# The second layer of eight tiles as seven products of quarters, in a fused attention and feed-forward kernel

## The chip, the cores and the metric

The kernel runs on one core of one Trainium2 chip. The time is device microseconds (us) of that core, the median over runs. The profile is one execution of the program, recorded on the chip; its lines give the engine (PE is TensorE's matmul, PEld its weight load, DVE VectorE, ACT ScalarE, POOL GpSimd, SP SyncE), the line of the kernel, the operation and its operands as "out<-in" by the program's names.

## The reference, cut to what matters

```python
def _attn_ref(q, k, v, g_norm):                 # q, k, v: 8 x 8 x 576 x 64
    kv = np.einsum('bhsd,bhse->bhde', k, v)
    out = np.einsum('bhsd,bhde->bhse', q, kv)
    rms = np.sqrt(np.mean(out * out, axis=-1, keepdims=True) + 1e-06)
    return out / rms * g_norm

def _moe_ref(x, w_in, w_out):                   # x: 4608 x 512, w_in: 512 x 2048, w_out: 2048 x 512
    h = x @ w_in
    g = h * (1.0 / (1.0 + np.exp(-1.702 * h)))
    return g @ w_out
```

The output of the attention, its heads side by side, is x: 8 batches of 576 rows with 512 columns. All of it is float32 outside; the kernel computes in float16 with float32 sums.

## The kernel before

**Tiles.** The 4608 rows go through the two layers in nine tiles of 512 rows: tile t (0 to 7) takes the first 512 rows of batch t, and tile 8 the 64 rows that are left of each of the eight batches, collected in `x_rem`. A tile has 16 blocks of 128 hidden columns. The first layer (`Hidden.mm`, L438) forms each block from four matmuls of 512 columns into a PSUM bank `hT`, and `gate` (L447, ScalarE) writes it as float16 into `gT`. The second layer (`project`, L475) then forms four blocks of 128 output rows, each from 16 matmuls: the weights loaded are a 128x128 piece of `gT`, the moving side is a row block of `w_out_sb` with 512 columns. So a tile is 64 matmuls and 64 matmuls. The bank of a finished block is copied to `osb` (L485) by ScalarE or VectorE and stored from there. In tile 8 the fourth block is split into 384 and 128 columns (`project_last`, L507).

**What lies in between.** While tile t is computed, the attention of batch t+1 is prepared in small units that `at1` hangs behind a block of the first layer and `at2` behind a numbered step of the second. For batches 2 to 7 they are: `cast_q` and the DMA transposes of q (`transpose_q`), `pack_k` (VectorE, L218), `kv` (TensorE, L227) with `keep_kv` (VectorE, L240), all in the first layer; then, in the second, `rows(0..3)` (four matmuls of 128 columns each, L291, a square on ScalarE, L299, a sum on VectorE, L302), `turn(0)` and `turn(2)` (for two row blocks each: Ln and Exp on ScalarE, L312 and L313; two multiplications `xr` on VectorE, L316, reading the banks of `rows`; one multiplication by g each on GpSimd and VectorE, L323; a DMA transpose on SP, L328, that writes half of the next tile's input `xT`), and `out`, `ss`, `apply` for the 64 left rows (L270, L339, L357). Tile 0 has a form of its own (`deep`), and batch 1 is prepared there in another way; tiles 7 and 8 prepare nothing.

**What sets the order.** Each engine works through its instructions in the order in which the kernel writes them, so a unit's place is where `at1` and `at2` put it. PSUM has three pools with a rotation each: `ps_h` (3 banks: `hT`, and `rows` 0 to 2), `ps_o` (2 banks: `o`) and `ps_a` (3 banks: `kvp` twice a tile, `rows` 3, `out`, `ss`). The next tile that is asked of a pool gets the bank that was given out longest ago, and the first writer waits for that bank's last reader. `gT` has one buffer, `osb` two. ScalarE has two table loads per tile: L653 ahead of the first Ln, and L447 ahead of the first gate.

The loop over the second layer's steps before is

```python
steps = [(mo, fo) for mo in range(4 - (t == B)) for fo in range(FO)]
for n, (mo, fo) in enumerate(steps):
    project(mo, fo)
    for u in units2.get(n, ()):
        u()
```

Of the kernel before, what the change touches and what calls it, by code (L numbers as in the profile page):

```python
# [7 lines left out]
F16 = mybir.dt.float16  # L8
# [4 lines left out]
P = 128  # L13
# [3 lines left out]
def kernel(  # L17
# [21 lines left out]
    R = S - SM  # L39
    assert R == 64 and B * R == SM and KO == NPAIR and 2 * D == P  # L40
    NT = B + 1
    LAST = ((0, 3 * P), (3 * P, DM))
    EARLY = 2
    PE_ = 96
    NJ = S // PE_
# [8 lines left out]
    attn = ctx.enter_context(tc.tile_pool(name="attn", bufs=4))  # L54
    xpool = ctx.enter_context(tc.tile_pool(name="xpool", bufs=2))
    gpool = ctx.enter_context(tc.tile_pool(name="gpool", bufs=1))
    opool = ctx.enter_context(tc.tile_pool(name="opool", bufs=2))
    ps_a = ctx.enter_context(tc.tile_pool(name="ps_a", bufs=3, space=bass.MemoryType.PSUM))
    ps_h = ctx.enter_context(tc.tile_pool(name="ps_h", bufs=3, space=bass.MemoryType.PSUM))
# [10 lines left out]
    kbuf = const.tile([P, NPAIR * NJ * P], F16)  # L70
# [9 lines left out]
    w_in_sb = const.tile([P, KO, DFF], F16)  # L80
    w_out_sb = const.tile([P, FO, DM], F16)
    x_rem = const.tile([P, KO, B * R], F16)


    raw = {"k": kraw, "q": qraw, "v": vbuf}
# [55 lines left out]

    first = {}
    for n in "kqv":
        first[n] = stage.tile([P, H, J * D], F32, name=f"{n}f", tag=f"{n}f")
        first[n] = first[n].rearrange("p h x -> p (h x)")[0:PE_, 0 : 2 * NJ * D]
# [283 lines left out]
    class Hidden:  # L429
# [16 lines left out]
        def gate(self, fo):  # L446
            nc.scalar.activation(self.gT[:, fo, :], self.h[fo], AFT.Gelu_apprx_sigmoid)  # L447

    def dense(t, units1, units2, group, deep, hid=None):
        hid = hid or Hidden(t)  # L450
        gT = hid.gT
        if group and t:
            order = [(ko, fo) for part in ((0, 3, 1, 2), range(4, group)) for ko in (0, 1) for fo in part]
            order += [(ko, fo) for ko in range(2, KO) for fo in range(group)]
            for ko, fo in order:
                pool = (ps_h, "hT") if fo < 3 else (ps_a, "att") if fo == 3 else (ps_o, "o")
                hid.mm(ko, fo, *pool)
            for fo in range(group):
                hid.gate(fo)
        for fo in range(FO):  # L460
            if fo >= group:
                for ko in range(KO):
                    hid.mm(ko, fo)
                hid.gate(fo)
            for u in units1.get(fo, ()):
                u()

        osb = osbs[t] = opool.tile([P, 4, DM], F32, name="osb", tag="osb")
        os = {}

        def project(mo, fo):
            if fo == 0:
                pool, tag = (ps_h, "hT") if deep and mo < 2 else (ps_o, "o")
                os[mo] = pool.tile([P, DM], F32, name="o", tag=tag)
            nc.tensor.matmul(  # L475
                os[mo],
                gT[:, fo, mo * P : (mo + 1) * P],
                w_out_sb[:, fo, :],
                start=(fo == 0),
                stop=(fo == FO - 1),  # L480
            )
            if fo == FO - 1:
                by_act = mo % 2 if deep or t == B else 0 < t < B - 1 and mo < 2
                copy = nc.scalar.copy if by_act else nc.vector.tensor_copy
                copy(osb[:, mo, :], os[mo])  # L485
                if t == B:
                    store_rest(mo, 0, DM)
                elif t in HALVED and mo % 2:
                    store(t, mo - 1, mo + 1)

        def store_rest(mo, n0, n1):
            for g in range(2):
                rows = out[(2 * mo + g) * S : (2 * mo + g + 1) * S, n0:n1]
                if 2 * mo + g < EARLY:
                    p0 = SM % PE_
                    rows = rows[bass.DynSlice(NJ * p0 + SM // PE_, R, step=NJ), :]
                else:
                    rows = rows[SM:S, :]
                queue = (nc.sync, nc.scalar)[g]
                queue.dma_start(out=rows, in_=osb[g * R : (g + 1) * R, mo, n0:n1])  # L500


        def project_last(mo):
            for i, (n0, n1) in enumerate(LAST):
                o = ps_a.tile([P, n1 - n0], F32, name="oh", tag="att")
                for fo in range(FO):
                    nc.tensor.matmul(  # L507
                        o,
                        gT[:, fo, mo * P : (mo + 1) * P],
                        w_out_sb[:, fo, n0:n1],  # L510
                        start=(fo == 0),
                        stop=(fo == FO - 1),
                    )
                copy = nc.vector.tensor_copy if i else nc.scalar.copy
                copy(osb[:, mo, n0:n1], o)  # L515
                store_rest(mo, n0, n1)

        if deep:
            steps = [(mo, 4 * i + k) for i in range(3) for mo in range(4) for k in range(4)]
            steps += [(mo, f + k) for f in (12, 14) for mo in range(2) for k in range(2)]  # L520
            steps += [(mo, 12 + k) for mo in (2, 3) for k in range(4)]
        else:
            steps = [(mo, fo) for mo in range(4 - (t == B)) for fo in range(FO)]
        for n, (mo, fo) in enumerate(steps):
            project(mo, fo)
            for u in units2.get(n, ()):
                u()
        if t == B:
            project_last(3)
# [115 lines left out]
    for t in range(NT):  # L645
# [12 lines left out]
        if t == 0:  # L658
            at1(7, of(0, "out", NPAIR))
            at2(4, setattr, a0, "ss_pool", Attention.ss_pool)  # L660
            at2(4, of(0, "ss", NPAIR, True))
            at2(4, of(0, "apply", NPAIR))
            at1(8, start, 1)
            for l in range(2):
                r = slice(l * PH, (l + 1) * PH)
                at1(8, nc.vector.memset, kpad[r, :, :, (1 - l) * D : (2 - l) * D], 0.0)
            for c in range(NPAIR):
                at1(12, of(1, "pack_q", c))
                at2(9 + 3 * c, of(1, "q", c))
# [63 lines left out]
```

## Time and profile before

| what | value |
|---|---|
| median of 3 runs | 286.75 us (286.32 to 287.19) |
| span of the profiled execution, first to last instruction | 285.4 us |
| its own time beside the span | not recorded apart; the runs' median is 1.35 above the span |
| granted TensorE clock | 1.000 |
| PE busy; the second layer's matmuls (L475); the first layer's (L438) | 278.8; 130.8; 116.4 and 14.0 us |
| VectorE, ScalarE, GpSimd busy | 119.2, 156.0, 59.5 us |
| second layer, tiles 1 to 6, first start to the next tile's first | 14.9 to 15.2 us each |
| second layer, tile 7 and tile 8 | 13.8 us each |

A row of the groups gives the line, engine, operation and operands, the count, then busy us and the mean ns of one, then the idle time of that engine just before these operations and what ended most of it. A row of a timeline gives start and duration in us of one instruction, or of several of one kind in a row (xN); the distance between their starts is shorter than one's duration, since matmuls are pipelined. A matmul of 512 columns has a record of 379 ns, while 64 of them in a row take 13.98 us. A figure in square brackets is idle time of the engine before the instruction, with what it waited for.

### The profile page before, as it was taken

The numbers are of one execution on the slowest core, as the hardware profiler recorded it, in microseconds if no ns is written. First come the engines' busy times: TensorE is split into PE (matmuls) and PEld (weight loads), VectorE is DVE, ScalarE is ACT, GpSimd is POOL, SyncE is SP. The second block draws the span as 40 slices with busy tenths as digits, with TensorE's granted clock in tenths as the row PEclk, the third lists the DMA queues.
The fourth block names the chain that finished last, engine by engine and source line by source line (L and its number), as shares of the span: only waits on it lengthen the run. The fifth ranks groups of instructions, "written<-read, shape, count | busy, mean of one in ns | idle before, by whom it ended". The sixth has DMA issues, their size and how long they took to land.

```text
span 285.4 us, 4458 instructions
## 1 busy us (share of the span) xinstructions
PE 278.8 (98%) x1768; PEld 136.9 (48%) x1768; DVE 119.2 (42%) x230; ACT 156.0 (55%) x273; POOL 59.5 (21%) x86
## 2 busy tenths in 40 slices
PE   8899999999999999999999999999999999999995
PEld 6444544455445544554455445544454444444443
DVE  2550547627661657147713852286327400110001
ACT  2688439766575645574467536763666365016400
POOL 8762372111211121112011401130001100000000
PEclk9999999999999999999999999999999999999999
DMA  8999999998579456963798269915401410012022
GB/s 174 192 198 205 205 235 239 208 262 158 127 168 249 73 128 175 238 95 62 208 207 161 41 209 230 161 37 184 85 0 37 117 69 0 2 60 87 0 75 75
DMA packets 55158, 38.78 MB, mean 136 GB/s; under 512 B 31282, under 2 KB 52018, under 8 KB 55010
## 3 DMA queue, kind: packets, MB, share of 16 engines
q0 software_dynamic: 16048, 15.59, 33.8%
q1 hardware_dynamic: 38688, 22.39, 30.5%
q10 hardware_dynamic: 402, 0.52, 0.6%
q8 instruction: 14, 0.23, 0.3%
q14 instruction: 6, 0.05, 0.1%
HBM read 36.73 MB, written 9.44 MB: 162 GB/s over the span
## 4 chain that ended last, share of the span: by engine, by line
PE 83%; DMA 13%; POOL 2%; issue 0%; DVE 0%
PE hT L438 39%; PE o L475 38%; DMA w_out_sb<-in_moe_w_out_dram 7%; DMA w_in_sb<-in_moe_w_in_dram 5%; PE kvp L227 2%; PE outR L291 2%; PE oh L507 1%; POOL qraw L91 1%; PE ss L339 0%; POOL kraw L91 0%; POOL vbuf L91 0%; PE outT L270 0%; PE outT L259 0%; DVE osb L515 0%; POOL ident L152 0%
## 5 line engine op out<-in xcount | busy, mean ns | idle before, releaser
L475 PE MATMUL o<-w_out_sb,gT 128*128 128x512 f16 x560 | 130.8, 379 | 0.1
L447 ACT ACTIVATE gT<-hT 128x512 f16<-128x512 f32 x144 | 84.5, 601 | 75.8 <-PE hT L438 75.8
L438 PE MATMUL hT<-xT,w_in_sb 128*128 128x512 f16 x512 | 116.4, 379 | 0.8 <-DMA w_in_sb<-in_moe_w_in_dram 0.8
L438 PEld LDWEIGHTS <-w_in_sb 128*128 128x128 f16 x576 | 54.6, 98 | 63.1 <-DMA w_in_sb<-in_moe_w_in_dram 1.1
L475 PEld LDWEIGHTS <-gT 128*128 128x128 f16 x560 | 52.9, 98 | 56.6 <-issue 0.4
L485 DVE COPY osb<-o 128x512 f32<-128x512 f32 x20 | 13.8, 691 | 62.4 <-PE o L475 62.4
L323 POOL TENSOR_TENSOR x<-xr,g_all 128x512 f16<-128x512 f32 x12 | 15.3, 1272 | 70.4 <-DVE xr L316 46.3
L218 DVE COPY kpad<-kraw 64x576 f16<-64x576 f16 x56 | 25.0, 446 | 2.4 <-DMA kraw<-in_k_dram 1.1
L240 DVE CAST kvb<-kvp 64x128 f16<-64x128 f32 x28 | 8.1, 289 | 39.1 <-PE kvp L227 38.9
L302 DVE TENSOR_REDUCE sum<-sq 128x8 f32<-128x512 f16 x24 | 15.8, 679 | 19.1 <-ACT sq L299 19.1
L112 POOL DMA_DIRECT2D kraw<-in_k_dram x16 | 10.0, 626 | 50.0 <-DVE kpad L218 34.5
L316 DVE TENSOR_TENSOR xr<-outR,sum 128x512 f32<-128x512 f32 x24 | 15.5, 686 | 11.1 <-ACT sum L313 11.1
L112 POOL DMA_DIRECT2D vbuf<-in_v_dram x16 | 9.7, 609 | 32.0 <-PE kvp L227 27.0
L323 DVE TENSOR_TENSOR x<-xr,g_all 128x512 f16<-128x512 f32 x12 | 15.2, 1268 | 0.7
L279 ACT ACTIVATE sq<-outT 128x512 f16<-128x512 f32 (+1 forms) x16 | 7.7, 488 | 13.2 <-PE outT L259 11.8
L299 ACT ACTIVATE sq<-outR 128x512 f16<-128x512 f32 x24 | 13.6, 590 | 2.0 <-PE outR L291 1.6
L227 PEld LDWEIGHTS <-kpad 128*128 128x128 f16 x252 | 11.0, 98 | 6.7 <-issue 0.6
L438 PE MATMUL hT<-x_rem,w_in_sb 128*128 128x512 f16 x64 | 14.0, 379 | 0.0
L485 ACT COPY osb<-o 128x512 f32<-128x512 f32 x15 | 8.7, 582 | 6.3 <-PE o L475 6.3
L227 PE MATMUL kvp<-vbuf,kpad 128*128 128x64 f16 x252 | 11.9, 193 | 0.1
L312 ACT ACTIVATE sum<-sum,eps_t 128x16 f32<-128x16 f32 x12 | 3.7, 308 | 15.0 <-DVE sum L302 15.0
L341 ACT ACTIVATE ln<-ss,eps_t 128x512 f32<-128x512 f32 (+1 forms) x16 | 9.4, 585 | 2.7 <-PE ss L339 2.6
(64 smaller groups left out, 145.1 us busy)
## 6 DMA issues: line engine op xcount, KB each, us to landing
qf<-in_q_dram SPq DMA_DIRECT2D x5, 1024.0 KB, 9.5
out_dram<-osb SPq DMA_DIRECT2D x10, 512.0 KB, 2.9
kraw<-in_k_dram POOLq DMA_DIRECT2D x12, 288.0 KB, 6.7
vbuf<-in_v_dram POOLq DMA_DIRECT2D x12, 288.0 KB, 5.8
out_dram<-osb SPq DMA_DIRECT2D x6, 192.0 KB, 6.0
w_in_sb<-in_moe_w_in_dram POOLq DMA_DIRECT2D x4, 256.0 KB, 7.7
w_out_sb<-in_moe_w_out_dram POOLq DMA_DIRECT2D x2, 512.0 KB, 14.5
w_out_sb<-in_moe_w_out_dram POOLq DMA_DIRECT2D x4, 256.0 KB, 10.6
```

The source lines that it names most:

```text
L112: nc.gpsimd.dma_start(out=raw[n][l * PH : (l + 1) * PH, c0:c1, 0 : NH * D], in_=srcs[n][b].rearrange("(c l) (p j) d -> l p c (j d)", l=2, ...
L218: nc.vector.tensor_copy(out=kpad[r, c, :, l * D : (l + 1) * D], in_=kraw[r, c, 0 : NH * D].rearrange("p (j d) -> p j d", j=NH),)
L227: nc.tensor.matmul(self.kvp[:, c, :], kpad[:, c, j, :], vbuf[:, c, j * D : (j + 1) * D], start=(j == 0), stop=(j == NH - 1),)
L299: nc.scalar.activation(sq, t, AFT.Square)
L302: nc.vector.tensor_reduce(out=self.sum2[:, j % 2, :], in_=sq.rearrange("p (h d) -> p h d", h=H), op=ALU.add, axis=mybir.AxisListType.X,)
L316: nc.vector.tensor_mul(xr[:, i], self.o[j + i].rearrange("p (h d) -> p h d", h=H), s2[:, i, :].unsqueeze(2).to_broadcast([P, H, D]),)
L323: (nc.vector if i else nc.gpsimd).tensor_mul(self.x16[:, j + i, :].rearrange("p (h d) -> p h d", h=H), xr[:, i], g_all.unsqueeze(1).to_bro ...
L341: nc.scalar.activation(ln[:, 0:n], t[:, 0:n], AFT.Ln, bias=eps_t, scale=1.0 / D)
L438: nc.tensor.matmul(self.h[fo], w_in_sb[:, ko, fo * P : (fo + 1) * P], self.x[:, ko], start=(ko == 0), stop=(ko == KO - 1),)
L447: nc.scalar.activation(self.gT[:, fo, :], self.h[fo], AFT.Gelu_apprx_sigmoid)
L475: nc.tensor.matmul(os[mo], gT[:, fo, mo * P : (mo + 1) * P], w_out_sb[:, fo, :], start=(fo == 0), stop=(fo == FO - 1),)
L485: copy(osb[:, mo, :], os[mo])
```

## The change

In tiles 1 to 8 the second layer is computed by Strassen's scheme in Winograd's form. `gT` is cut into quarters (hidden blocks 0 to 7 and 8 to 15, rows 0 to 255 and 256 to 511), `w_out_sb` likewise (hidden blocks, and columns 0 to 255 and 256 to 511). Instead of eight products of quarters there are seven, each of 16 matmuls with 256 moving columns: 112 matmuls per tile. They need sums of quarters as operands. Those of `w_out` (`tw`, four of 128x2048) are formed once, on VectorE in tile 1 (`weight_sums`); those of `gT` (`gS`, four of 128x2048 per tile) on VectorE in three portions behind blocks 8, 12 and 15 of the first layer, whose blocks now come in the order 0, 8, 1, 9 and so on. The products go in the order 1, 5, 6, 2, 7, 3, 4 into three banks: x (products 1, 6, 7, 4, one on top of the other), z (5 and 3) and y (2). After products 1, 5 and 6 the partial sum is copied to SBUF by ScalarE (`s1`, `s5`, `s2`); after 2, 7 and 3 VectorE adds one of these copies to the bank and writes a quarter of the output; after 4 ScalarE copies the last quarter. x and z are from `ps_o`, y from `ps_a`, so that in tiles 2 to 6 a tile takes six banks from `ps_a` instead of five. A unit that hung behind step n now hangs behind step 7n/4, rounded down. In tile 8 x is two half tiles, one of them from `ps_a`, and the stores of a whole output row block follow products 7 and 3. In tile 0 the code of the second layer stays as it was. The first loads of q, k and v share two staging buffers, and an unused one (`kbuf`) goes.

```diff
-    LAST = ((0, 3 * P), (3 * P, DM))
+    spool = ctx.enter_context(tc.tile_pool(name="spool", bufs=1))
+    HF, HN = FO // 2, DM // 2
+    tw = const.tile([P, 4, HF, HN], F16)
...
+    def weight_sums():
+        b11, b12 = w_out_sb[:, 0:HF, 0:HN], w_out_sb[:, 0:HF, HN:DM]
+        b21, b22 = w_out_sb[:, HF:FO, 0:HN], w_out_sb[:, HF:FO, HN:DM]
+        sub = nc.vector.tensor_sub
+        sub(tw[:, 0], b12, b11)
+        sub(tw[:, 1], b22, tw[:, 0])
+        sub(tw[:, 2], b22, b12)
+        sub(tw[:, 3], b21, tw[:, 1])
...
+        def sums(self, i0, i1):
+            lo, hi = slice(i0, i1), slice(HF + i0, HF + i1)
+            r1, r2 = slice(0, 2 * P), slice(2 * P, SM)
+            g, s = self.gT, self.s
+            nc.vector.tensor_add(s[:, 0, lo], g[:, lo, r2], g[:, hi, r2])
+            nc.vector.tensor_sub(s[:, 1, lo], s[:, 0, lo], g[:, lo, r1])
+            nc.vector.tensor_sub(s[:, 2, lo], g[:, lo, r1], g[:, lo, r2])
+            nc.vector.tensor_sub(s[:, 3, lo], g[:, hi, r1], s[:, 1, lo])
...
+                1: (self.gT[:, i, rows], w[:, i, 0:HN]),
+                2: (self.gT[:, HF + i, rows], w[:, HF + i, 0:HN]),
+                3: (self.s[:, 3, i, rows], w[:, HF + i, HN:DM]),
+                4: (self.gT[:, HF + i, lower], tw[:, 3, i]),
+                5: (self.s[:, 0, i, rows], tw[:, 0, i]),
+                6: (self.s[:, 1, i, rows], tw[:, 1, i]),
+                7: (self.s[:, 2, i, rows], tw[:, 2, i]),
...
+                pool, tag = (ps_a, "att") if name == "y" or key[1] else (ps_o, "o")
+                n = 1 if split else 2
+                self.bank[key] = pool.tile([P, n, HN], F32, name="o7", tag=tag)
...
+        def keep(self, name, as_):
+            t = self.kept[as_] = attn.tile([P, 2, HN], F32, name=as_, tag=as_, bufs=1)
+            for ps, m in self.whole(name):
+                nc.scalar.copy(t[:, m], ps)
...
+                if with_:
+                    nc.vector.tensor_add(o[:, m], ps, self.kept[with_][:, m])
+                else:
+                    nc.scalar.copy(o[:, m], ps)
+                    if self.t == B:
+                        store_rest(2 * i + m.start, j * HN, (j + 1) * HN)
...
+        def run(self, units2):
+            n = 0
+            for p in self.ORDER:
+                name = {1: "x", 6: "x", 7: "x", 4: "x", 2: "y", 5: "z", 3: "z"}[p]
...
+                        if mo and i == HF - 1:
+                            self.after(p)
+                        for u in units2.get(n, ()):
+                            u()
+                        n += 1
...
+            if p == 1:
+                self.keep("x", "s1")
+            elif p == 5:
+                self.keep("z", "s5")
+            elif p == 6:
+                self.keep("x", "s2")
+            elif p == 2:
+                self.place("y", "s1", 0, 0)
+            elif p == 7:
+                self.place("x", "s5", 1, 1)
+                if t == B:
+                    store_rest(2, HN, DM)
+                    store_rest(3, HN, DM)
+            elif p == 3:
+                self.place("z", "s2", 0, 1)
+                if t == B:
+                    store_rest(0, 0, DM)
+                    store_rest(1, 0, DM)
+                elif t in HALVED:
+                    store(t, 0, 2)
+            else:
+                self.place("x", None, 1, 0)
+                if t in HALVED:
+                    store(t, 2, J)
...
+        seven = None if deep else Seven(t, gT)
+        cols = range(FO) if deep else [f for i in range(HF) for f in (i, HF + i)]
+        ready = {} if deep else {8: (0, 4), 12: (4, 6), 15: (6, 8)}
...
+            if i in ready:
+                seven.sums(*ready[i])
+            for u in units1.get(i, ()):
                 u()
...
+            later = {}
+            for n, us in units2.items():
+                later.setdefault(n * 7 // 4, []).extend(us)
+            seven.run(later)
...
             if t == 1:
+                at1(5, weight_sums)
```

More of the change, by code (lines that the diff above doesn't have):

```diff
@@ L69 @@
     qrem = [const.tile([P, 2, P], F16, name=f"qrem{i}") for i in range(2)]
-    kbuf = const.tile([P, NPAIR * NJ * P], F16)
     qbuf = const.tile([P, NPAIR * NJ * P], F16)
@@ L143 @@
     for n in "kqv":
-        first[n] = stage.tile([P, H, J * D], F32, name=f"{n}f", tag=f"{n}f")
-        first[n] = first[n].rearrange("p h x -> p (h x)")[0:PE_, 0 : 2 * NJ * D]
+        if n != "q":
+            rows = stage.tile([P, H, J * D], F32, name="qf", tag="qf")
+            rows = rows.rearrange("p h x -> p (h x)")[0:PE_]
+        first[n] = rows[:, (n == "q") * 2 * NJ * D :][:, 0 : 2 * NJ * D]
         dst, src = first[n].rearrange("p (h x) -> p h x", h=2), early_src(n, 0, 0, 1)
@@ L447, in gate, with __init__, operands, banks @@
             nc.scalar.activation(self.gT[:, fo, :], self.h[fo], AFT.Gelu_apprx_sigmoid)
+    def weight_sums():
[6 more added lines that the diff above has]
+        sub(tw[:, 3], b21, tw[:, 1])
+    class Seven:
+        ORDER = (1, 5, 6, 2, 7, 3, 4)
+        def __init__(self, t, gT):
+            self.t, self.gT = t, gT
+            self.s = spool.tile([P, 4, HF, 2 * P], F16, name="gS", tag="gS")
+            self.bank, self.kept = {}, {}
+        def sums(self, i0, i1):
[6 more added lines that the diff above has]
+            nc.vector.tensor_sub(s[:, 3, lo], g[:, hi, r1], s[:, 1, lo])
+        def operands(self, p, mo, i):
+            rows = slice(mo * P, (mo + 1) * P)
+            lower = slice((2 + mo) * P, (3 + mo) * P)
+            w = w_out_sb
+            return {
+                1: (self.gT[:, i, rows], w[:, i, 0:HN]),
[5 more added lines that the diff above has]
+                7: (self.s[:, 2, i, rows], tw[:, 2, i]),
+            }[p]
+        def banks(self, name, mo):
+            split = self.t == B and name == "x"
+            key = (name, mo if split else 0)
+            if key not in self.bank:
+                pool, tag = (ps_a, "att") if name == "y" or key[1] else (ps_o, "o")
+                n = 1 if split else 2
+                self.bank[key] = pool.tile([P, n, HN], F32, name="o7", tag=tag)
+            return self.bank[key][:, 0 if split else mo]
+        def whole(self, name):
+            return [
+                (self.bank[k], slice(k[1], k[1] + self.bank[k].shape[1]))
+                for k in sorted(self.bank)
+                if k[0] == name
+            ]
+        def keep(self, name, as_):
+            t = self.kept[as_] = attn.tile([P, 2, HN], F32, name=as_, tag=as_, bufs=1)
+            for ps, m in self.whole(name):
+                nc.scalar.copy(t[:, m], ps)
+        def place(self, name, with_, i, j):
+            o = osbs[self.t][:, 2 * i : 2 * i + 2, j * HN : (j + 1) * HN]
+            for ps, m in self.whole(name):
+                if with_:
[8 more added lines that the diff above has]
+                name = {1: "x", 6: "x", 7: "x", 4: "x", 2: "y", 5: "z", 3: "z"}[p]
+                split = self.t == B and name == "x"
+                for mo in range(2):
+                    o = self.banks(name, mo)
+                    for i in range(HF):
+                        a, w = self.operands(p, mo, i)
+                        nc.tensor.matmul(
+                            o,
+                            a,
+                            w,
+                            start=(p in (1, 2, 5) and i == 0 and (mo == 0 or split)),
+                            stop=(i == HF - 1),
+                            skip_group_check=True,
+                        )
+                        if mo and i == HF - 1:
[3 more added lines that the diff above has]
+                        n += 1
+        def after(self, p):
+            t = self.t
+            if p == 1:
[22 more added lines that the diff above has]
+                    store(t, 2, J)
@@ L449, in dense, with store_rest @@
+    def store_rest(mo, n0, n1):
+        osb = osbs[B]
+        for g in range(2):
+            rows = out[(2 * mo + g) * S : (2 * mo + g + 1) * S, n0:n1]
+            if 2 * mo + g < EARLY:
+                p0 = SM % PE_
+                rows = rows[bass.DynSlice(NJ * p0 + SM // PE_, R, step=NJ), :]
+            else:
+                rows = rows[SM:S, :]
+            queue = (nc.sync, nc.scalar)[g]
+            queue.dma_start(out=rows, in_=osb[g * R : (g + 1) * R, mo, n0:n1])
     def dense(t, units1, units2, group, deep, hid=None):
@@ L454, in dense @@
             order += [(ko, fo) for ko in range(2, KO) for fo in range(group)]
[L455 to L461, printed above, removed]
+            for ko, i in order:
+                pool = (ps_h, "hT") if i < 3 else (ps_a, "att") if i == 3 else (ps_o, "o")
+                hid.mm(ko, cols[i], *pool)
+            for i in range(group):
+                hid.gate(cols[i])
+        for i, fo in enumerate(cols):
+            if i >= group:
                 for ko in range(KO):
@@ L464, in dense @@
                 hid.gate(fo)
-            for u in units1.get(fo, ()):
+            if i in ready:
+                seven.sums(*ready[i])
+            for u in units1.get(i, ()):
                 u()
@@ L472, in project @@
             if fo == 0:
-                pool, tag = (ps_h, "hT") if deep and mo < 2 else (ps_o, "o")
+                pool, tag = (ps_h, "hT") if mo < 2 else (ps_o, "o")
                 os[mo] = pool.tile([P, DM], F32, name="o", tag=tag)
@@ L482, in project @@
             if fo == FO - 1:
-                by_act = mo % 2 if deep or t == B else 0 < t < B - 1 and mo < 2
-                copy = nc.scalar.copy if by_act else nc.vector.tensor_copy
+                copy = nc.scalar.copy if mo % 2 else nc.vector.tensor_copy
                 copy(osb[:, mo, :], os[mo])
[L486 to L516, printed above, removed]
         if deep:
@@ L521, in dense @@
             steps += [(mo, 12 + k) for mo in (2, 3) for k in range(4)]
-        else:
[L523 to L529, printed above, removed]
+            for n, (mo, fo) in enumerate(steps):
+                project(mo, fo)
+                for u in units2.get(n, ()):
+                    u()
+        else:
+            later = {}
+            for n, us in units2.items():
+                later.setdefault(n * 7 // 4, []).extend(us)
+            seven.run(later)
         if t < EARLY:
```

## The prediction

> **What bounds the kernel now.** I read the page first: busy times, then the costliest groups.
>
> ```profile
> PE 278.8 (98%) x1768; PEld 136.9 (48%) x1768; DVE 119.2 (42%) x230; ACT 156.0 (55%) x273; POOL 59.5 (21%) x86
> ...
> L475 PE MATMUL o<-w_out_sb,gT 128*128 128x512 f16 x560 | 130.8, 379 | 0.1
> ...
> L291 PE MATMUL outR<-kvb,qTd 128*128 128x128 f16 x96 | 9.3, 219 | 0.0
> ```
>
> TensorE is busy in 98% of the span, and the second layer (L475) never waits (0.1 us idle). The price of a matmul is the distance between starts, which the timeline of PE gives. First tile 3 (which prepares batch 4) from its second layer's first to the next tile's first matmul, then tile 7 (which prepares no later batch) and the last product (start, duration, engine, line, times):
>
> ```profile
> 122.08 0.59 PE L475 MATMUL o<-w_out_sb,gT 128*128 128x512 f16 x2
> 122.51 0.39 PE L291 MATMUL outR<-kvb,qTd 128*128 128x128 f16 x4
> ...
> 131.11 0.27 PE L339 MATMUL ss<-sq,ones 128*128 128x256 f16 x1
> ...
> 137.04 2.32 PE L438 MATMUL hT<-xT,w_in_sb 128*128 128x512 f16 x10
> ...
> 240.32 13.98 PE L475 MATMUL o<-w_out_sb,gT 128*128 128x512 f16 x64
> ...
> 278.31 3.66 PE L507 MATMUL oh<-w_out_sb,gT 128*128 128x384 f16 x32
> ```
>
> 64 matmuls in 13.98, less the last one's record of 0.379: 13.60/63 = 0.216 us each. Four with 128 columns, every one with its own weight load: (0.39-0.219)/3 = 0.057. The last row holds 16 with 384 and 16 with 128 columns: 3.66-0.22 = 3.44 = 16a+15x0.057, a = 0.162. 256 lies midway: 0.109. So width sets the price, and the weight load hides.
>
> Tile 3 spends 137.04-122.08 = 14.96 us in the second layer: 64x0.216 = 13.82, and 1.1 for four `rows`, `out` and `ss`. Beside it runs a chain that prepares the next tile's input; the timelines of ACT and of DVE show it:
>
> ```profile
> 122.28 0.60 ACT L447 ACTIVATE gT<-hT 128x512 f16<-128x512 f32 x1 [0.27 <-PE hT L438]
> ...
> 124.42 1.28 ACT L653 ACT_TABLE_LOAD   x1
> 125.72 0.31 ACT L312 ACTIVATE sum<-sum,eps_t 128x16 f32<-128x16 f32 x1
> ...
> 126.18 1.06 ACT L299 ACTIVATE sq<-outR 128x512 f16<-128x512 f32 x2
> ...
> 130.23 0.31 ACT L312 ACTIVATE sum<-sum,eps_t 128x16 f32<-128x16 f32 x1 [2.51 <-DVE sum L302]
> ...
> 130.69 0.36 ACT L279 ACTIVATE sq<-outT 128x256 f16<-128x256 f32 x1
> ```
> ```profile
> 124.44 0.69 DVE L302 TENSOR_REDUCE sum<-sq 128x8 f32<-128x512 f16 x1 [0.18 <-ACT sq L299]
> 126.36 1.29 DVE L316 TENSOR_TENSOR xr<-outR,sum 128x512 f32<-128x512 f32 x2 [1.24 <-ACT sum L313]
> 127.74 1.27 DVE L323 TENSOR_TENSOR x<-xr,g_all 128x512 f16<-128x512 f32 x1
> 128.93 1.27 DVE L302 TENSOR_REDUCE sum<-sq 128x8 f32<-128x512 f16 x2
> 130.82 1.29 DVE L316 TENSOR_TENSOR xr<-outR,sum 128x512 f32<-128x512 f32 x2 [0.62 <-ACT sum L313]
> 132.14 1.27 DVE L323 TENSOR_TENSOR x<-xr,g_all 128x512 f16<-128x512 f32 x1
> ```
>
> Call the first Ln (125.72) X. The second follows at X+4.51, the second `xr` pair ends at X+6.39 (130.82+1.29), the last x16 multiply at X+7.69 (132.14+1.27). Then the transposes (L328) land 3.1 us later by the trace's landing times: 136.5, only 0.5 ahead of the next tile at 137.04. So in tiles 1 to 6 TensorE runs hardly ahead of a chain of waits, and an edit that shortens TensorE's work meets it at once.
>
> **What the change removes.** Per tile 64x0.216 = 13.82 us of matmul becomes 112x0.109 = 12.23: -1.6. In tiles 7 and 8, which have no such chain, I take all of it: each PSUM copy (0.58 to 0.69 here) has a product of 16x0.109 = 1.75 us before its bank is written again. **Tiles 7 and 8: -3.2.** Six more tiles at -1.6 would make -12.8 in all; I do not expect it.
>
> The Trainium skill speaks against the change here: "TensorE: Matmul & The Clock Gate", section Back-to-back issue gap, gives some 81 ns per pair of weight load and matmul at 128 columns and 131 at 512. On a straight line 256 would be 98, and 112x98 = 11.0 against 64x131 = 8.4 an estimated loss of 2.6 us per tile. The rows above (57 and 216) do not agree with it.
>
> **The operand sums on VectorE.** The trace has no f16 `tensor_tensor` with both inputs in SBUF. Upper bound: one element at a time as in the f32 copies (128 columns 0.292, 512 columns 0.691: 1.04 ns each and 0.16 fixed), 0.69 for 512. Lower bound: the f16 copy of 96x768 in 0.374. I take the rate of the f16 copy L218 (576 in 0.446: 0.5 ns each), the nearest in type: 0.42 for 512, 0.67 for 1024, 1.18 for 2048. The Trainium skill, "VectorE: DVE Perf Modes", section The perf-mode tier table, gives 1224 ns for a 16-bit one of 2048; the sum by it would be the same within 0.5 us. No trace shown so far has it.
>
> **One tile of 2 to 6**, in us from the start of its second layer, in queue order:
> - The last gate ends at 0.8 (122.88). The third set of four sums follows, 1.6 with the gaps, and then both reduces (1.27, now behind the sums on VectorE): X = 3.7, against 3.64 before. Bounds: 3.4 (the table load, which comes a little earlier because `rows` do) and 4.7 (sums at 0.69).
> - ACT's order is now: two squares, table load, Ln, Exp, a square, **s1**, a square, Ln, Exp, **s5**, **s2**, the square of `out`. s1 stands behind Ln, at X+0.93 (before, a third ACT operation would have started there), done at 5.2. Product 6 writes the bank that s1 reads and is due at 32x0.109+4x0.22 = 4.4: it waits 0.8. Then product 6, `out`, product 2: 5.2+1.75+0.12+1.75 = 8.8.
> - The matmul of `ss` is next on TensorE. With y in the same pool, a tile now takes six banks from `ps_a` instead of five, and `ss` gets the bank of the fourth `rows`, which the second `xr` reads last. In the built order its weight load waits for that `xr`: X+6.39 = 10.1. It also waits for the square of `out`, behind s5 and s2: X+4.51+0.46+2x0.47+0.36 = 10.0. So TensorE stands until 10.15, 1.35 more, with products 7, 3 and 4 queued behind.
> - ss 0.11 and 48x0.109 = 5.24: the layer ends at **15.5**. VectorE has placed product 7 by 13.1, before product 4 needs its bank at 13.75. The transposes land at X+10.85 = 14.6, in time.
> - The last copy (product 4) is now on ACT, and the gelu table load of 1.28 behind it: 0.2+0.58+1.28, first gate done 2.7 into the next tile, where TensorE has filled three banks at 12x0.216 = 2.6: 0.1.
>
> 15.5-14.96+0.14 = +0.68; **five tiles: +3.4.**
>
> **Tile 1** also gets the weight sums ahead of its casts and `kpad` copies: 4x1.18 = 4.8 from 49.4 on. Casts and copies (1.4+3.6) end at 59.1 instead of 55.6, the first sums (2.5) at 61.6, the second (1.5) at 63.1; the two `keep_kv` (before at 59.3 and 61.6) come after them, at 64.3, and `rows`, due at 62.46, waits 1.9 for them. Then X is 5.35 into the layer and `ss` 11.8; the end is 17.4 (with the second `out` and `ss`) against 77.40-62.24 = 15.16. **+2.4** with the gate. If the cover (55.6 to 62.4) were longer, this would be nothing. The queues take it: GpSimd's next k load goes out 3.5 later (59) and lands in 6.7, for a use at 79.5; on SP the eight stores of tile 1 start only with the last placings and hold the next q transposes back some 1.5, which are issued at 79.7, land in 4.5 and are needed at 92.7.
>
> **The end.** Before, the last copy is followed by one store on each queue. Now two whole-row stores of products 2 and 3 are issued on ACT (0.49 to 0.67 each in the trace) between product 3 and the last copies, and one more between these two: VectorE is done 0.85 before the last matmul, the two issues take until +0.3, copy 0.38, issue 0.5, copy 0.38; the last store starts at +1.7 instead of +0.5, and 64 KB land in 2.3 instead of 1.9. **+1.5**, bounds 0.4 and 2.
>
> Sum: -3.2+3.4+2.4+1.5 = **+4.1 us**, 289.5 on the profiled span of 285.4. What lies around the span (286.75-285.4 = 1.35) I leave as it is: **290.8 us**, 1.4% slower.
>
> **Rivals.**
> - *The chain gives way* (faster). Mechanism: `ss` gets its bank earlier. The sum is nil if it starts by 9.3 instead of 10.15; at best the transposes become the bound (14.6, -0.36 per tile): 5x(-0.36)+1.3-3.2+1.5 = -2.2, **284.5**. For it: 98% busy TensorE. Against it: every piece of the chain has a row, and X can be no more than 0.3 earlier. 0.10.
> - *Sums at one element at a time* (0.69, 1.22, 2.28 us). Then X is 5.0, since `keep_kv` after the second sums holds `rows` by 1 us: the layer is 16.9, +2.1 per tile of five, +6 to 8 in tile 1: **301**. Nothing in the trace excludes it but the faster f16 copies. 0.08.
> - *Half the width costs more than half.* Midway between 0.109 and the 0.162 of 384 columns, 0.136, products cost 15.2 per tile: tiles 7 and 8 lose 1.4 each instead, and 48 matmuls after `ss` add 1.3 in six tiles: **304**. It pays only below 13.82/112 = 0.123. The skill's rule above points this way; the rows do not. 0.02.
> - *My forecast*, 0.80. With X at 3.4, no wait for the gate, 1 us less in tile 1 and 1 at the end it would be 287.2; with the waits 0.3 longer per tile and tile 1 at +4, 294.5.
>
> **The numbers.** Range 286.5 to 295: the forecast's own, a little over its low end; the 301, 304 and most of the 284.5 case stay out. Faster or slower by over 0.3% (0.86 us, about what a measurement of this kernel can tell from no change): in my case 0.72 slower, 0.06 within, 0.02 faster; with the rivals slower 0.82, same 0.07, faster 0.11.
>
> **What would show it.** In tiles 2 to 6: PE idle of some 0.8 ahead of product 6, released by ACT, and 1.3 ahead of `ss`, released by DVE `xr` or ACT; second layers of 15.5, of 12.2 in tiles 7 and 8; `gS` operations of 0.42 and 0.67; matmuls with 256 columns 0.109 apart. I am wrong if those waits are missing, or if the sums take 0.69.

## The result, and the profile after

The changed kernel takes 291.15 us (median of 4 runs, 290.25 to 291.50) against 286.88 (286.32 to 287.19) in the same comparison: a ratio of 1.0144, 95% interval 1.0123 to 1.0164, slower by some 1.4%. The profiled execution spans 288.9 us (before 285.4) at a granted clock of 0.996. The forecast was 290.8.

The page, busy times and then groups:

```profile
PE 269.0 (93%) x2136; PEld 172.9 (60%) x2136; DVE 169.6 (59%) x336; ACT 165.3 (57%) x294; POOL 59.7 (21%) x86
...
L534 PE MATMUL o<-tw,gS 128*128 128x256 f16 x384 | 46.5, 272 | 3.6 <-ACT s L513 3.6
```

TensorE has 9.8 us less to do than before, and the span is 3.5 longer: the share fell from 98% to 93%. TensorE now stands, and the second row already names one thing that it stands for: ScalarE's copy of a partial sum. The table of PE's waits (us in all, times, longest) lists the rest; the three largest rows are all in the second layer:

```profile
PE ss L342 <- DVE xr L319: 6.5, 6, 1.1
PE o L534 <- ACT s L513: 3.6, 6, 0.6
PE outR L294 <- DVE kvb L243: 1.4, 2, 1.1
```

"6 times" means once in each of the tiles 1 to 6, those that prepare a later batch. The third row is tile 1 alone. In the same table of the kernel before, `ss` waited 0.2 us, once, and `o` and `outR` not at all. Where the waits are shows PE's timeline of tile 3:

```profile
124.42 0.38 PE L534 MATMUL o<-w_out_sb,gT 128*128 128x256 f16 x2
...
127.50 1.47 PE L534 MATMUL o<-tw,gS 128*128 128x256 f16 x12
129.59 1.91 PE L534 MATMUL o<-tw,gS 128*128 128x256 f16 x16 [0.62 <-ACT s L513]
131.34 0.28 PE L273 MATMUL outT<-qTr,kvb 128*128 128x64 f16 x4
131.45 1.91 PE L534 MATMUL o<-w_out_sb,gT 128*128 128x256 f16 x16
134.47 0.28 PE L342 MATMUL ss<-sq,ones 128*128 128x256 f16 x1 [1.11 <-DVE xr L319]
134.59 1.91 PE L534 MATMUL o<-tw,gS 128*128 128x256 f16 x16
...
139.83 1.46 PE L441 MATMUL hT<-xT,w_in_sb 128*128 128x512 f16 x6
```

16 matmuls of 256 columns are due every 16x0.109 = 1.74 us. Product 6 was due at 127.50+12x0.109 = 128.81 and starts at 129.59: it comes 0.78 late. `ss` was due at 131.45+1.74 = 133.19 and starts at 134.47: 1.28 late. (The figure in brackets is 0.16 smaller, because the record of a matmul of 256 columns is 0.272 long while the next one may start after 0.109: lost time is read from starts.) The layer takes 139.83-124.42 = 15.41 us. Seven products and the attention's matmuls alone would take 12.23+1.1 = 13.33; the two waits are the rest: 13.33+0.78+1.28 = 15.39.

ScalarE's timeline in the same tile says why:

```profile
126.55 1.28 ACT L765 ACT_TABLE_LOAD   x1
128.03 0.31 ACT L315 ACTIVATE sum<-sum,eps_t 128x16 f32<-128x16 f32 x1 [0.19 <-DVE sum L305]
...
128.97 0.58 ACT L513 COPY s<-o 128x512 f32<-128x512 f32 x1
...
132.54 0.31 ACT L315 ACTIVATE sum<-sum,eps_t 128x16 f32<-128x16 f32 x1 [2.50 <-DVE sum L305]
133.00 1.05 ACT L513 COPY s<-o 128x512 f32<-128x512 f32 x2
133.94 0.40 ACT L282 ACTIVATE sq<-outT 128x256 f16<-128x256 f32 x1
```

The copy s1 (128.97) stands in ScalarE's queue behind the first Ln (128.03), and product 6 writes the bank that s1 reads. Then ScalarE sits idle 2.50 for VectorE's sums ahead of the second Ln (132.54), and s5, s2 and the square of `out`, which `ss` needs, are queued behind that Ln; the square ends at 134.34. VectorE's second pair of `xr`, the last readers of the bank that `ss` gets, ends at about the same time:

```profile
126.72 1.27 DVE L305 TENSOR_REDUCE sum<-sq 128x8 f32<-128x512 f16 x2
...
133.12 1.29 DVE L319 TENSOR_TENSOR xr<-outR,sum 128x512 f32<-128x512 f32 x2 [0.62 <-ACT sum L316]
134.45 1.26 DVE L326 TENSOR_TENSOR x<-xr,g_all 128x512 f16<-128x512 f32 x1
```

`ss` has two releasers within 0.1 us of each other (134.41 and 134.34). The view names one. Whether either alone would have held it is a question for an experiment.

Where the 3.5 us came from, from starts in the two traces:

| part | before | after | difference | forecast |
|---|---|---|---|---|
| second layer of tile 1 | 15.16 | 17.21 | +2.05 | +2.2, and 0.1 for the gate |
| second layer of tiles 2 to 6, each | 14.96 | 15.41 | +0.45 | +0.54 |
| first layer of tiles 3 to 7, each (gate behind the last copy) | 14.86 (tile 7: 13.81) | 15.02 (13.97) | +0.16 | +0.14 |
| second layer of tile 7 | 13.81 | 12.23 | -1.58 | -1.6 |
| last matmul's start to the end of the span | 3.62 | 5.66 | +2.04 | +1.5 |

The second layer of tile 8 gets another 1.7 shorter, from its first to its last matmul's start, and tile 1's began 0.3 earlier. That start is scatter: the first layer of tile 1 began at 47.38 in the kernel before, at 47.04 here, and anywhere from 46.64 to 47.70 in the profiled executions of the runs below.

### The profile page after: what moved, and what is told of

Read it like the earlier page. It is cut to its first block, busy times and chain, and to the rows that moved or that the text cites. A ratio compares the mean times of both kernels' runs of the same rounds, so it can differ in the third digit from the quotient of the medians.

```text
span 288.9 us, 5327 instructions
## 1 busy us (share of the span) xinstructions
PE 269.0 (93%) x2136; PEld 172.9 (60%) x2136; DVE 169.6 (59%) x336; ACT 165.3 (57%) x294; POOL 59.7 (21%) x86
## 5 line engine op out<-in xcount | busy, mean ns | idle before, releaser
L534 PEld LDWEIGHTS <-gS 128*128 128x128 f16 x512 | 49.8, 98 | 10.1 <-issue 4.6
L534 PE MATMUL o<-tw,gS 128*128 128x256 f16 x384 | 46.5, 272 | 3.6 <-ACT s L513 3.6
L475 DVE TENSOR_TENSOR gS<-gT 128x512 f16<-128x512 f16 (+1 forms) x24 | 12.3, 514 | 53.9 <-ACT gT L450 53.8
L534 PEld LDWEIGHTS <-gT 128*128 128x128 f16 x384 | 36.7, 98 | 5.6
L534 PE MATMUL o<-w_out_sb,gT 128*128 128x256 f16 x256 | 33.5, 273 | 0.0
L519 DVE TENSOR_TENSOR osb<-o,s 128x512 f32<-128x512 f32 (+1 forms) x25 | 16.6, 662 | 18.6 <-issue 9.7
L319 DVE TENSOR_TENSOR xr<-outR,sum 128x512 f32<-128x512 f32 x24 | 15.5, 686 | 8.1 <-ACT sum L316 8.1
L513 ACT COPY s<-o 128x512 f32<-128x512 f32 (+1 forms) x26 | 13.6, 547 | 6.4 <-PE o L534 6.4
L618 PE MATMUL o<-w_out_sb,gT 128*128 128x512 f16 x64 | 16.7, 379 | 0.0
L534 PE MATMUL o<-w_out_sb,gS 128*128 128x256 f16 x128 | 15.5, 273 | 0.0
L534 PE MATMUL o<-tw,gT 128*128 128x256 f16 x128 | 15.3, 273 | 0.0
```

Of the source, the lines that this page charges most:

```text
L319: nc.vector.tensor_mul(xr[:, i], self.o[j + i].rearrange("p (h d) -> p h d", h=H), s2[:, i, :].unsqueeze(2).to_broadcast([P, H, D]),)
L513: nc.scalar.copy(t[:, m], ps)
L519: nc.vector.tensor_add(o[:, m], ps, self.kept[with_][:, m])
L534: nc.tensor.matmul(o, a, w, start=(p in (1, 2, 5) and i == 0 and (mo == 0 or split)), stop=(i == HF - 1), skip_group_check=True,)
L618: nc.tensor.matmul(os[mo], gT[:, fo, mo * P : (mo + 1) * P], w_out_sb[:, fo, :], start=(fo == 0), stop=(fo == FO - 1),)
```

## The experiments

Beside each kernel, the kernel before ran on the same chip; ratios are to that. The changed kernel did not run again beside them, so a difference to its 291.15 us is one between two comparisons; times of layers are read from the traces.

**Is it the bank or the queue that holds `ss`?** The first edit takes y's bank from `ps_h`, so that `ss` no longer gets the bank that `xr` reads; ScalarE's order stays.

```diff
-                pool, tag = (ps_a, "att") if name == "y" or key[1] else (ps_o, "o")
+                pool, tag = (ps_h, "hT") if name == "y" else (ps_a, "att") if key[1] else (ps_o, "o")
```

> y gets its bank from ps_h instead of ps_a; the matmul of ss then no longer gets the bank that the second xr reads. My theory: two waits end almost together there, the bank at 10.1 and ScalarE's square of out (behind s5 and s2, behind the second Ln) at 10.0; so only 0.1 per tile comes off, layers of 15.3 in tiles 2 to 6 and 290.5 us. Rival, the bank alone is the cause: the whole wait of 1.1 goes in six tiles, layers of 14.3, 284.5 us.

290.28 us, 1.0094 [1.0063, 1.0125]; the layer of tile 3 took 15.32. The wait stays and has a new name (PE's waits of this kernel):

```profile
PE ss L342 <- ACT sq L282: 6.1, 6, 1.0
PE o L534 <- ACT s L513: 3.6, 6, 0.6
```

The bank alone was not it. The second edit leaves the bank and moves the second `turn` behind `out`, so that s5, s2 and the square no longer stand behind the second Ln:

```diff
-            at2(16, of(b, "turn", 2))
             at2(27, of(b, "out", NPAIR))
+            at2(27, of(b, "turn", 2))
```

> turn(2) is written behind s2 and the square of out instead of ahead of s5, so that ScalarE copies s5 and s2 before it stands at the second Ln; y stays in ps_a. My theory: ss still waits for the bank that the second xr reads, 10.1 into the layer, so nothing moves: 15.4 and 291 us. Rival, the copies behind Ln are the cause: ss starts at 8.9, layers of 14.5 or less, 286 us or less.

291.54 us, 1.0167 [1.0095, 1.0239], layers of 15.41: nothing, and the row of the wait is that of the changed kernel.

```profile
PE ss L342 <- DVE xr L319: 6.5, 6, 1.1
```

The third has both edits.

> Both of the edits before. My theory: ss starts at 8.9, right behind product 2; what is late next is VectorE, which places product 7 only behind its last multiplication by g, at 12.9 instead of the 12.4 at which product 4 needs the bank, so the layer ends at 14.7 instead of 15.4: -0.7 in six tiles, 287 us. Rival, the chain of waits has another binding member (the transposes at the tile's end): 290 or more. Rival, nothing is late next: layers of 14.2, 284 us.

286.65 us, 0.9977 [0.9957, 0.9997]: the loss is gone, and most layers of tiles 2 to 6 are 14.68 (tiles 4 and 5: 15.02 and 14.86; in tile 4 the next first layer already waits for the transposes that write `xT`, 0.18 us by the bracket). So `ss` had two holders, either of which was enough, and an edit of one shows almost nothing. What is left, in the waits of this kernel and in its timeline of tile 3:

```profile
PE o L534 <- ACT s L513: 3.6, 6, 0.6
PE o L534 <- DVE osb L519: 1.9, 5, 0.4
```
```profile
135.67 1.91 PE L534 MATMUL o<-tw,gT 128*128 128x256 f16 x16 [0.39 <-DVE osb L519]
```

The wait for s1 is unchanged, and product 4 now waits for VectorE to place product 7 (0.55 by starts), since VectorE is still with the two `xr` and the multiply by g. 13.33+0.79+0.55 = 14.67.

**Is the attention's chain on VectorE what stretches the layer?** Here the multiplication by g of batches 2 to 7 is left out in the changed kernel (`xr` is written to `x16` directly, four VectorE and GpSimd operations of 512 fewer per tile); the next does the same to the kernel before.

```diff
-                    xr[:, i],
+                    self.x16[:, j + i, :].rearrange("p (h d) -> p h d", h=H),
...
-            for i in range(2):
-
-                (nc.vector if i else nc.gpsimd).tensor_mul(
...
```

> The changed kernel without the multiplication by g for batches 2 to 7 (left out: xr writes x16 itself). It shortens the chain by about 1.3 twice and leaves TensorE's work alone. My theory: the second Ln comes at X+2.7, ss is no longer waited for, only product 6 still waits 0.7 for s1; layers of 14.15 in tiles 2 to 6, -1.2 in six tiles, 283.5 us, below the kernel before. Rival, the seven products or their copies themselves cost the time: layers stay at 15.4, 291 us.

> The kernel before without the multiplication by g for batches 2 to 7 (left out as in the run on the changed kernel). My theory: TensorE never waits there, so a shorter chain beside it is worth nothing: 287 us, within 0.5. Rival, the multiplications themselves or what they keep busy cost time in either kernel, and the gain seen without g belongs to them and not to the chain: 3 us or more below, 284 us or less.

The changed kernel goes to 284.13 us, 0.990 [0.985, 0.995], with layers of 14.13 (tile 5: 14.34): `ss` doesn't wait any more, and of the two only the wait for s1 is left (3.8 us in six tiles, 0.8 at most):

```profile
PE o L526 <- ACT s L505: 3.8, 6, 0.8
```

The kernel before stays without the multiplications: 287.19 us, 1.0022 [0.9997, 1.0047], layer 14.93 against 14.96. So the chain cost the old kernel nothing, and it is the new one that TensorE meets it in. Shortening the chain in this way is worth 7 us after the change and nothing ahead of it.

**The weight sums in tile 1.** Left out here are the sums of `w_out` (pieces of `w_out_sb` stand in for `tw`), with all else in place.

```diff
-                5: (self.s[:, 0, i, rows], tw[:, 0, i]),
+                5: (self.s[:, 0, i, rows], w[:, i, HN:DM]),
...
-                at1(5, weight_sums)
```

> The sums of w_out are left out (plain pieces of w_out stand in their place, so the output is not the reference's). My theory: VectorE is 4.8 us less late in tile 1, rows no longer wait for keep_kv, and tile 1's second layer takes 15.65 instead of 17.2: 289.5 us. Rival, tile 1 is long for another reason (its second out and ss, the group of blocks at its start): no change, 291.1 us.

289.78 us, 1.0123 [1.007, 1.0176]; the second layer of tile 1 takes 15.66 instead of 17.21, and the waits of `outR` for `kvb` are gone. The sums cost 1.55 us in tile 1's layer. The medians differ by 1.4, but the ratio's interval holds the changed kernel's 1.0144, so it is the trace that shows this.

**The end.** The last two copies of tile 8 go from ScalarE, where they stand among the issues of stores, to VectorE.

```diff
-                    nc.scalar.copy(o[:, m], ps)
+                    copy = nc.vector.tensor_copy if self.t == B else nc.scalar.copy
+                    copy(o[:, m], ps)
```

> In tile 8 the last two copies go to VectorE, so that they no longer stand behind the stores that ScalarE issues. My theory: the last copy ends at 0.6 after the last matmul instead of 1.9, the last store starts 0.4 to 0.9 earlier (ScalarE's own last issue is then what is late): 290.3 us. Rival, the stores' transfers set the end: no change, 291.1 us.

The time missed its expectation: 291.07 us, 1.0153 [1.0128, 1.0179]. In the trace the end, last matmul's start to the end of the span, fell from 5.66 to 5.20, and ScalarE's last issue came 1.42 behind that matmul instead of 2.12; but in that execution tile 1 started 0.66 later and its second layer took 0.30 longer, which hid the 0.46. The four times lie between 290.73 and 292.01, too far apart to tell 0.46, so it rests on one trace of each kernel. This is the end of the changed kernel, all engines:

```profile
281.61 1.91 PE L534 MATMUL o<-tw,gT 128*128 128x256 f16 x16
...
282.53 1.39 ACTq L585 DMA_DIRECT2D out_dram<-osb  x2
284.02 0.37 ACT L521 COPY osb<-o 128x256 f32<-128x256 f32 x1 [7.08 <-PE o L534]
284.42 0.50 ACTq L585 DMA_DIRECT2D out_dram<-osb  x1
284.96 0.37 ACT L521 COPY osb<-o 128x256 f32<-128x256 f32 x1 [0.57 <-ACT osb L521]
285.36 0.50 ACTq L585 DMA_DIRECT2D out_dram<-osb  x1
```

The last matmul starts at 283.24. The first last copy waits for two issues ahead of it (282.53 to 283.92), the second for an issue between them, as forecast; the last issue comes 2.12 behind that matmul.

**A version from these findings.** It has y in `ps_h`, g folded once into a copy `w_in_g` of the first layer's weights (four VectorE operations in tile 0; no multiplication by g in tiles 1 to 6, and the left rows scaled by ones), the first `turn` behind s1, the second behind `out`, the last quarter copied by VectorE, and two of the weight sums behind tile 1's first `turn`. It computes the whole reference.

```diff
+            for ko in range(KO):
+                at1(8, nc.vector.tensor_scalar_mul, w_in_g[:, ko], w_in_sb[:, ko], g_col)
...
+            at2(9, of(b, "turn", 0))
+            if t == 1:
+                at2(9, weight_sums, 1)
             for j in range(J):
-                at2((1, 4, 8, 11)[j], of(b, "rows", j))
-            at2(7, of(b, "turn", 0))
-            at2(16, of(b, "turn", 2))
+                at2((1, 4, 9, 11)[j], of(b, "rows", j))
             at2(27, of(b, "out", NPAIR))
+            at2(27, of(b, "turn", 2))
...
-                    nc.scalar.copy(o[:, m], ps)
+                    nc.vector.tensor_copy(o[:, m], ps)
```

> A version that should beat both: g is multiplied into a second copy of w_in once (VectorE, while it waits in tile 0), so the multiplication by g leaves the chain; y from ps_h; s1 ahead of the first Ln, s5, s2 and the square of out ahead of the second; the last quarter copied by VectorE, so the gelu table is loaded in time; half of the weight sums behind turn(0) in tile 1. My theory: no wait of TensorE is left in tiles 2 to 6, layers of 13.4, and the first layers back at 14.86; 276 us, 11 below the kernel before. Rival, another chain takes over as the waits did in the changed kernel (VectorE's placings ahead of product 4, or its casts at the tile's start): layers of 14 or more, 280 us or more.

277.23 us, 0.9666 [0.9652, 0.9681]: 9.7 us below the kernel before on its chip. Page, and PE's timeline of tile 3:

```profile
PE 265.6 (96%) x2136; PEld 173.6 (63%) x2136; DVE 163.7 (59%) x338; ACT 161.7 (59%) x285; POOL 42.2 (15%) x73
```
```profile
119.87 0.38 PE L531 MATMUL o<-w_out_sb,gT 128*128 128x256 f16 x2
...
122.95 3.22 PE L531 MATMUL o<-tw,gS 128*128 128x256 f16 x28
...
126.12 1.91 PE L531 MATMUL o<-w_out_sb,gT 128*128 128x256 f16 x16
127.87 0.27 PE L336 MATMUL ss<-sq,ones 128*128 128x256 f16 x1
127.98 1.91 PE L531 MATMUL o<-tw,gS 128*128 128x256 f16 x16
...
133.22 2.97 PE L436 MATMUL hT<-xT,w_in_g 128*128 128x512 f16 x13
```

No brackets are left in tile 3; products 5 and 6 run as one row of 28, and the layer is 133.22-119.87 = 13.35, the sum of its matmuls. First layers are 14.86 again, and tile 1's second layer is 14.61, with 0.7 us of waits left in the brackets. This is what the seven products are worth when next to nothing waits; the shorter chain by itself brought the kernel before nothing (287.19 us above). The version makes several edits at once. That s1 alone, written ahead of the first Ln, ends the wait of product 6 is read from the queue's order and from the missing wait here; no run moved it alone.

**What sets the new end.** In that version the end is still 5.63 (last matmul's start 269.82, span 275.45) although the copies were moved. Two theories were left: the stores are issued late, or their transfer takes that long. First, in the row blocks 1 to 3 of tile 8 each pair of 64-row stores became one of 2x64 rows, on this version and on the one with VectorE's last copies:

```diff
+            rows = out.rearrange("(b s) n -> b s n", s=S)[2 * mo : 2 * mo + 2, SM:S, n0:n1]
+            queue.dma_start(out=rows, in_=osb[:, mo, n0:n1])
```

> The folded version with one store of 128 partitions instead of two of 64 for the row blocks 1 to 3 of tile 8 (7 stores instead of 12). If the issue of stores on ScalarE's and SP's queues is what is late at the end (my theory after the run on the last copies), the time from the last matmul's start to the span's end falls from 5.6 to 4.7 or less: 276.3 us. If the transfers or the order in which they land set the end, it stays at 5.6 and 277.2 us.

> The same seven stores in the changed kernel with its last copies on VectorE. Issue of stores is late: from the last matmul's start to the span's end 4.7 instead of 5.7 in the changed kernel and 5.2 with the copies alone, 290.2 us. Transfers set the end: 5.2 or more, 291 us.

290.14 us, 1.008 [1.0043, 1.0117], and 303.12 us, 1.0564 [1.0519, 1.0609]: 13 and 12 slower than the same kernels without it. The edit changed something else. Busy us of the engines by stretch, then clock, DMA share and GB/s, in the first of the two:

```profile
276.00:280.00 4.00, 0.00 (x0) 0.00 (x0) 0.00 (x0) 0.00 (x0) 0.00 (x0) 0.50 0.13 48
```

A share of 0.13 is 2 of 16 DMA engines: the stores with an outer size of 2 went out on two engines at 48 GB/s in all. The Trainium skill, "DMA: Bandwidth & Descriptors", section "Why a DMA increments its semaphore by 16 and not by 1", has a rule for this: the number of engines is the largest up to 16 that divides, in both access patterns, the size of the slowest dimension longer than 1. With 2 that is two, and the trace agrees. So these two runs say nothing about the theories. Then the two stores behind product 3 went from ScalarE's queue to GpSimd's:

```diff
-            queue = (nc.sync, nc.scalar)[g]
+            queue = (nc.sync, nc.gpsimd if mo < 2 else nc.scalar)[g]
```

> The folded version with ScalarE's two stores behind product 3 issued by GpSimd instead, still 64 partitions each, so that ScalarE has only the stores of products 7 and 4 to issue. If the issue queues are late at the end, the last issue comes at 1.5 or less after the last matmul's start instead of 2.0 and the span ends 0.4 to 0.8 earlier: 5.0 instead of 5.6 behind the last matmul, 276.7 us. If transfers or their landing set the end, or GpSimd's issue is no quicker: 5.6, 277.2 us.

277.18 us, 0.9647 [0.9628, 0.9666], span 275.4: no change, and the end is 5.72 instead of 5.63 behind the last matmul's start (269.68). ScalarE's last issue came 0.77 behind that start instead of 1.95, so ScalarE's issues do not set the end of the best version. But SP's queue got no shorter: its last issue starts 1.51 behind that start and lasts 1.16, so the last issue of all ends 2.67 behind it, where it ended 2.51 behind in the best version. Here are the issues that start last, ScalarE's in the best version and SP's in this one:

```profile
271.77 0.56 ACTq L582 DMA_DIRECT2D out_dram<-osb  x1
```
```profile
271.19 1.16 SPq L582 DMA_DIRECT2D out_dram<-osb  x1
```

What speaks for the transfer are the 2 us behind the last matmul, in the kernel before, in the best version and in the one with GpSimd's issues:

```profile
281.50:283.50 2.00, 0.47 (x9) 0.29 (x6) 0.29 (x1) 0.09 (x1) 0.00 (x0) 1.00 0.35 94
```
```profile
270.00:272.00 2.00, 0.09 (x1) 0.00 (x0) 0.42 (x1) 0.00 (x0) 0.00 (x0) 1.00 0.88 238
```
```profile
270.00:272.00 2.00, 0.00 (x0) 0.00 (x0) 0.41 (x1) 0.00 (x0) 0.33 (x1) 1.00 0.91 210
```

The 16 DMA engines are busy 88 to 91% of that time, against 35% before. The scheme finishes its quarters late: 768 KB of tile 8's 1 MB are stored only behind products 7, 3 and 4, although the quarter of product 2 is ready earlier and waits for product 3 to make whole rows. At 238 GB/s 768 KB are 3.3 us. Against it: in the best version the next 2 us show a share of 0.53, and the last 1.4 us move nothing, so the engines are nearly full for about 2 of the 5.63 us.

```profile
272.00:274.00 2.00, 0.00 (x0) 0.00 (x0) 0.00 (x0) 0.00 (x0) 0.00 (x0) 1.00 0.53 162
274.00:275.40 1.40, 0.00 (x0) 0.00 (x0) 0.00 (x0) 0.00 (x0) 0.00 (x0) 0.76 0.00 0
```

No run shortened both queues of issues, and none took bytes away from the end. What sets the new end stays open.

## Why the prediction was right

- **Half the width costs half.** Forecast 0.109 us per matmul of 256 columns; measured 0.109 between starts. Tile 7 came out at 12.23, as worked out. The rival of half width at more than half fell. So did the estimate of 98 ns, on a straight line between the figures of the Trainium skill ("TensorE: Matmul & The Clock Gate", section "Back-to-back issue gap") for 128 and 512 columns.
- **The operand sums.** Forecast 0.42, 0.67 and 1.18 us. The rows of `gS`, shapes apart, are

```profile
L475 DVE TENSOR_TENSOR gS<-gT 128x512 f16<-128x512 f16 x16 | 6.8, 425 | 18.9 <-ACT gT L450 18.8
L475 DVE TENSOR_TENSOR gS<-gT 128x1024 f16<-128x1024 f16 x8 | 5.5, 692 | 35.0 <-ACT gT L450 35.0
```

  and `tw` took 1.21 to 1.23. That is (692-425)/512 = 0.52 ns per element, and the rival of one element at a time (1.04) fell. The 1224 ns that the Trainium skill ("VectorE: DVE Perf Modes", section "The perf-mode tier table") gives for bfloat16 agree to 1%.
- **Product 6 behind s1.** X was forecast at 3.7 and is 128.03-124.42 = 3.61; the wait was forecast at 0.8 and is 0.78.
- **`ss` behind the second `xr` and behind the square of `out`.** Forecast 10.1 and 10.0 into the layer, a wait of 1.35; measured 9.99 and 9.92, and 1.28. The first three experiments showed both holders to be real, and each to be enough. The layer: 15.5 forecast, 15.41 measured. The rival in which the chain gives way fell with it: it needed `ss` by 9.3.
- **The gate behind the last copy**: 0.14 forecast with five tiles, 0.16 measured.
- **Tile 1**: 17.4 forecast, 17.21 measured. VectorE ran in the forecast order, 0.4 to 0.5 earlier than written, of which 0.3 is the earlier start: the weight sums began at 48.9 instead of 49.4, and `keep_kv` ended at 63.9 instead of 64.3. Without the weight sums the layer is 15.66.
- **The end** is the term that was mis-sized: +2.04 (5.66 less 3.62), just over its upper bound of 2, for +1.5. The queue of issues and copies on ScalarE was as described, but slower: the two issues ahead of the first last copy lasted until 0.68 behind the last matmul's start (forecast 0.3), and the last issue came at 2.12 instead of 0.58, so 1.54 later (forecast 1.2). The other 0.50 lie behind that issue (forecast 0.4 for a slower landing). With the copies on VectorE 0.46 came back in one trace; what holds the rest is open.
- **The sum.** +4.1 forecast for the span, +3.5 measured: tile 1 0.3 less, five tiles 0.4 less in all, tiles 7 and 8 0.1 less, the end 0.5 more, and 0.3 by the earlier start of tile 1, which is scatter.
- **Luck.** The time came within 0.4 us of 290.8, nearer than the span. The prediction left 1.35 us around the span as it was, but that is the median of three runs less the span of one: in the runs of the kernel before whose span is on record, time and span lie 1.72 to 1.89 apart. In the changed kernel the median lies 2.25 above the profiled span. The 0.9 missing here and the 0.6 too much in the span offset each other in part.
- **Two sums beside the forecast** come out otherwise by their own terms. The rival of slow sums gives 301.5 to 303.5 rather than 301 (-3.2, 5x2.1, 6 to 8 and 1.5 on 286.75), and the low end of the forecast some 286.6 rather than 287.2 (1.5 for X and 0.7 for the gate in five tiles, 1 and 1), still inside the range. Neither touches the forecast.

What the prediction didn't say is how little the loss depends on the scheme. It named the chain as the bound, but priced no edit that would shorten it; the same seven products with the chain out of the way gain 3.3%.

## What to carry to other kernels

Saving work on the busiest engine pays only as far as the next chain of waits, so price that chain to its end before the edit, and ask for each new copy which queue it stands in and who needs the bank that it frees. When an instruction has two releasers within a tenth of a microsecond, an edit of one can show next to nothing, as it did here: try both together before giving up on either. A scheme that completes its outputs late moves their stores into the tail, where nothing hides them.

## What the runs showed of the hardware that was not expected

Stores of 2x64 rows of 1 or 2 KB used two of the 16 DMA engines (share 0.13, 48 GB/s) and added 12 to 13 us to the end, while stores of 64 rows each kept nearly all of them busy (0.88, 238 GB/s). Matmuls of 256 columns with a weight load each went at 0.109 us, so that halving the width cost TensorE nothing, though weight loads rose from 136.9 to 172.9 us.
